# An FFT and two expert layers on one core: half of the first stage's input without halves, its loads joined, the first weight loaded earlier

## The chip, the core and the metric

The kernel runs on one core of a Trainium2 chip. The core has five engines that run beside each other and meet through semaphores: PE (TensorE, the matmuls; PEld are its weight loads), DVE (VectorE), ACT (ScalarE), POOL (GpSimd) and SP (SyncE, which here only issues DMAs). The metric is device time in microseconds; lower is better.

## What is computed

An FFT over tokens and features of x, of which the real part is kept, goes through two expert layers one behind the other, all in float32:

```python
X = np.fft.fft(np.fft.fft(x, axis=1), axis=2).real      # x: 2 x 3008 x 256
h = X.reshape(6016, 256) @ w_in                         # w_in: 256 x 2048
g = np.maximum(h, 0.0) + alpha * np.minimum(h, 0.0)
Y = g @ w_out                                           # w_out: 2048 x 256
h = Y @ w_in2
out = (h / (1.0 + np.exp(-h))) @ w_out2
```

## The kernel before, in words

The FFT over 3008 = 47 x 64 tokens is done in two stages. Stage A is a product with the table `cat` over 47 points. Its result goes through DRAM (`tmid`), which turns it, and stage B is a product with `cbt` over 64 points. The FFT over features is folded into the first weight: `mix_w` multiplies `w_in` with the table `cwt` and gives `wa`. The tokens that come out are cut in six groups c = 0 to 5. The body then runs 16 steps for each group (`step1`: product with `wa`, activation, product with `wo1`) and then the second layer in the same manner. A plan written out by hand (lists of step numbers such as STAGE_A, STAGE_B, WOUT) says at which step what side work is issued; the instructions of each engine run in the order in which the program issues them.

Products use a fast float32 format (float32r) of lower precision. To keep float32, an operand is split: `hi` is a rounded copy (ACT), `lo` is the rest (DVE or POOL), and three matmuls give hi x hi, lo x hi and hi x lo. An operand that stays plain float32 needs no halves and one matmul; psB, psW and psP are made so.

The change lies in the prologue for group 0, ahead of step 1. It goes thus:

- PE runs ten idle matmuls on zeros (`spin(SPIN[0])`). SP issues the loads of x in eight parts `xr[i]` of 96 x 1024 and of the table `ca`.
- For each part i: `split` makes xh (ACT) and xl (DVE) one part ahead, `stage_a` does two halves of three matmuls each (L304 to L306), ACT copies the first half out of PSUM to `evs[i]`, DVE the second (L893, L895). Then the entry `QUEUE[i]` says which DMAs follow: "s" saves rows of tmid for the first third (L313), "l" loads rows back into `ur` (L846; the name pq in the trace, since ur lies in pq of the last group), "w" and "b" load the tables cwt and cbt from ACT's queue, "p" begins the conversion of a first-layer weight: it issues its load (L165), and the next `next(first[0])` its ACT steps (L193, L194) and DVE steps (L199, L201, L203), which turn a pair of 32-bit words into a float32. "o" loads a raw w_out.
- `ur` holds 128 partitions; the even rows (e = 0) and the odd rows (e = 1) of a part are loaded by DMAs of their own, the odd ones in two large DMAs at the end.
- Behind the stage: 14 idle matmuls, the mixing of weight 0 (psW, L452, and psS, L458), 8 idle matmuls, stage B for group 0 (psB, L917: eight products for the even rows, then eight for the odd ones), the row product of POOL (L912) and its sum on PE (psP, L928), the conversion of weight 1, and step 1 (psh, L495).

SP issues in order: while a DMA waits for a semaphore, all that stand behind it wait too. A load waits until the saves that it reads have landed.

Of the kernel before, what the change touches and what calls it, by code (L numbers as in the profile page):

```python
# [9 lines left out]
F32 = mybir.dt.float32  # L10
# [4 lines left out]
ALU = mybir.AluOpType  # L15
# [7 lines left out]
NP1 = 48  # L23
# [4 lines left out]
CK = 8  # L28
# [49 lines left out]
def kernel(  # L78
# [13 lines left out]
    nc = tc.nc  # L92
    V, A, G, T = nc.vector, nc.scalar, nc.gpsimd, nc.tensor
# [206 lines left out]
    def stage_a(hi, lo, tag="x"):  # L300

        t = ptile([P, 4, P], "psA", tag)
        ps = t[:2 * NP1]
        T.matmul(ps, cat[:, 0, :], hi, start=True, stop=False)  # L304
        T.matmul(ps, cat[:, 1, :], hi, start=False, stop=False)
        T.matmul(ps, cat[:, 0, :], lo, start=False, stop=True)  # L306
        return ps
# [455 lines left out]
    def start_win2():  # L763
# [15 lines left out]
    T2 = 14, 16, 19, 22, 50, 51, 52, 53, 54, 56, 58  # L779
    SUB = G  # L780
    STEP2 = [0] + [NC * NF + 56 * c for c in range(NC - 1)]
    SPIN = 10, 14, 8

    QUEUE = ((("s", 0, 8),), (("s", 8, 16),), (("s", 16, 24), ("w",), ("b",)), (("s", 24, 32), ("p", 0)),
             (("l", 0, 16, 0), ("s", 32, 40)), (("l", 16, 32, 0), ("s", 40, 48)), (("s", 48, 56), ("l", 32, 48, 0)),
             (("s", 56, 60), ("s", 60, 64), ("l", 48, 56, 0), ("l", 56, 64, 0), ("l", 0, 32, 1), ("l", 32, 64, 1),
              ("a",), ("p", 1), ("o",)))
    FIRST = 6
    WARM = {}

    RAWS = {"o0": (0, "wA2"), "o1": (1, "wA2"), "i2": (0, "px1"), "i3": (1, "px1"), "i4": (0, "wA3"), "i5": (1, "wA3"),
# [9 lines left out]
    with tc.manual_schedule():  # L801
# [39 lines left out]

        first = [narrow_win(p) for p in range(2)]

        def load_ur(a, b, e):
            dst = ur[2 * a:2 * b, e * CK:(e + 1) * CK]
            nc.sync.dma_start(dst, tmid[0][a:b].rearrange("n (c e m) j -> (n c) e m j", c=2, e=2)[:, e])  # L846

        def save(a, b):
            i = a // NX
# [3 lines left out]
        def move(what):  # L853
            kind, *at = what
            if kind == "s":
                save(*at)
            elif kind == "l":
                load_ur(*at)
            elif kind == "w":
                A.dma_start(cwt.rearrange("p k e j -> p (k e j)"), cw)  # L860
            elif kind == "b":
                A.dma_start(cbt.rearrange("p e k -> p (e k)"), cb)
            elif kind == "a":
                nc.sync.dma_start(al, alpha)
            elif kind == "p":
                next(first[at[0]])
            elif kind == "o":
                load_raw("o", 0)

        sp = {}  # L870

        def split(i):
            hi = wtile([2 * NP1, NX, P], F32R, "xh0", "gh")
            lo = wtile([2 * NP1, NX, P], F32R, "xl0", "gl")
            A.activation(hi, xr[i], AF.Copy)
            V.tensor_tensor(lo, xr[i], f32(hi), op=ALU.subtract)
            sp[i] = hi, lo

        V.tensor_copy(*con)
        split(0)  # L880
        evs = []
        for i in range(nx):
            if i + 1 < nx:
                split(i + 1)
            if i % 2 == 0:
                t = keep.tile([2 * NP1, 2, NX, P], F32, name="ev0", tag=("px2", "px3", "px4", "px6")[i // 2])
            evs.append(t[:, i % 2])
            hi, lo = sp.pop(i)
            for h in range(2):
                sl = slice(h * 4, h * 4 + 4)  # L890
                ps = stage_a(hi[:, sl], lo[:, sl], "x" if (2 * i + h) % 4 == 3 else "h")
                if h == 0:
                    A.activation(evs[i][:, sl], ps, AF.Copy)  # L893
                else:
                    V.tensor_copy(evs[i][:, sl], ps)  # L895
            for what in QUEUE[i]:
                move(what)
            if i == FIRST:
                next(first[0])
# [166 lines left out]
```

## Time and profile before

| | us |
|---|---|
| median of 3 runs | 994.22 |
| lowest, highest | 994.04, 995.43 |
| the profiled execution | 997.01 |
| its span, first to last instruction | 995.2 |

The profile is of one execution of its own, a little longer than the median. The page gives the busy time of each engine; the timeline gives each instruction's start (us from the span's start), its duration, and in brackets how long its engine stood idle before it and what released it. A matmul's end is modelled, so the distance between two starts tells more than a duration. DMAs show when they were issued, and in the view of DMA issues how long until they landed.

### The profile page before, as it was taken

Reading aid. Unit: us, or ns where it says so; the run is one execution under the profiler, and the core shown is the slowest. Engines: PE = TensorE matmul, PEld = TensorE weight load, DVE = VectorE, ACT = ScalarE, POOL = GpSimd, SP = SyncE. Lnnn points to the kernel's source line nnn. Section 1 sums busy time; section 2 is a strip of 40 time slices with the busy share of each in tenths; the row PEclk is TensorE's granted clock in tenths of the full one; section 3 lists DMA queues with packets and bytes.
Section 4 is the critical chain, followed back from the end, with each engine's and each line's share of the span. In section 5 each row is a group of like instructions: output and inputs, shape, how many; then the busy total and the mean of one; then the engine's idle time right before and its main releaser. Section 6 shows DMA issues by size and latency. Waiting matters only on the chain. (4 is left out here: it accounts for less than half of the span.)

```text
span 995.2 us, 12396 instructions
## 1 busy us (share of the span) xinstructions
PE 963.0 (97%) x4316; PEld 792.8 (80%) x4316; DVE 733.0 (74%) x1103; ACT 597.1 (60%) x1002; POOL 519.3 (52%) x328
## 2 busy tenths in 40 slices
PE   8799999999999999999999999999999999999998
PEld 5677778878888878777787788888888888888886
DVE  6698877678777789988999875576566566657654
ACT  6566566665555556666787666565565566566554
POOL 0155657765545556887987654254253354335222
PEclk9899999999999999999999999999999999999999
DMA  8921123221011010110122020000001001001001
GB/s 224 318 83 38 41 75 90 76 63 51 1 53 54 1 53 22 42 64 26 39 68 81 1 82 1 1 22 22 1 1 43 1 1 40 1 0 43 1 1 43
DMA packets 35950, 46.43 MB, mean 47 GB/s; under 512 B 3408, under 2 KB 22192, under 8 KB 35632
## 3 DMA queue, kind: packets, MB, share of 16 engines
q1 hardware_dynamic: 35600, 45.32, 14.6%
q8 instruction: 34, 0.56, 0.2%
q10 hardware_dynamic: 288, 0.33, 0.1%
q14 instruction: 28, 0.23, 0.1%
HBM read 32.11 MB, written 13.52 MB: 46 GB/s over the span
## 5 line engine op out<-in xcount | busy, mean ns | idle before, releaser
L679 DVE TENSOR_TENSOR ring<-ring,psh 128x512 f32<-128x512 f32 (+1 forms) x336 | 221.7, 674 | 154.2 <-PE psh L658 141.2
L726 PE MATMUL pso<-ghl,wAo 128*128 128x512 f32 (+1 forms) x1152 | 312.3, 387 | 1.7 <-POOL ghl L670 1.7
L525 POOL TENSOR_TENSOR gl<-r,gh 128x1024 fp32r<-128x1024 f32 (+1 forms) x96 | 231.5, 2412 | 150.2 <-ACT gh L524 107.0
L658 PE MATMUL psh<-ts,wi 128*128 128x512 f32 (+1 forms) x1008 | 281.4, 387 | 2.5 <-DVE ring L679 1.5
L670 POOL TENSOR_TENSOR ghl<-ring,ghl 128x512 fp32r<-128x512 f32 (+1 forms) x96 | 139.3, 1451 | 249.6 <-ACT ghl L665 169.9
L726 PEld LDWEIGHTS pso<-ghl,wAo 128*128 128x128 f32 x1152 | 216.7, 188 | 44.9 <-POOL ghl L670 2.5
L682 ACT ACTIVATE ring<-ring 128x512 f32<-128x512 f32 (+1 forms) x192 | 119.5, 623 | 173.6 <-DVE ring L679 171.6
L658 PEld LDWEIGHTS psh<-ts,wi 128*128 128x128 f32 x1008 | 189.3, 188 | 40.4 <-DVE ring L679 2.2
L540 PE MATMUL pso<-gh,wo_o 128*128 128x512 f32 (+1 forms) x768 | 189.8, 388 | 2.4 <-POOL wo_o L221 2.3
L495 PE MATMUL psh<-pq,wa 128*128 128x512 f32 (+1 forms) x576 | 168.1, 400 | 5.6 <-DVE r L509 5.5
L540 PEld LDWEIGHTS pso<-gh,wo_o 128*128 128x128 f32 x768 | 144.2, 188 | 32.2 <-POOL wo_o L221 4.0
L509 DVE SCALAR_TENSOR_TENSOR r<-r,al,psh 128x512 f32<-128x512 f32 (+1 forms) x192 | 132.9, 734 | 15.7 <-ACT r L505 4.6
L524 ACT ACTIVATE gh<-r 128x1024 fp32r<-128x1024 f32 (+1 forms) x96 | 100.3, 1045 | 65.0 <-DVE r L509 64.6
L495 PEld LDWEIGHTS psh<-pq,wa 128*128 128x128 f32 x576 | 105.2, 189 | 30.9 <-DVE r L509 11.9
L665 ACT ACTIVATE ghl<-ring 128x512 fp32r<-128x512 f32 (+1 forms) x192 | 119.1, 620 | 6.3 <-PE psh L658 0.4
L505 ACT ACTIVATE r<-psh 128x512 f32<-128x512 f32 (+1 forms) x96 | 56.5, 589 | 94.9 <-DVE psh L504 94.9
L504 DVE TENSOR_TENSOR psh<-h,psh 128x512 f32<-128x512 f32 (+1 forms) x96 | 65.9, 686 | 55.5 <-PE psh L495 51.5
L540 PE MATMUL pso<-gl,wo_o 128*128 128x512 f32 (+1 forms) x384 | 104.0, 392 | 2.4 <-POOL gl L525 2.4
L540 PEld LDWEIGHTS pso<-gl,wo_o 128*128 128x128 f32 x384 | 72.5, 190 | 18.5 <-POOL gl L525 4.1
L670 DVE TENSOR_TENSOR ghl<-ring,ghl 128x512 fp32r<-128x512 f32 (+1 forms) x96 | 76.8, 800 | 2.7 <-ACT ghl L665 2.7
L503 DVE SCALAR_TENSOR_TENSOR h<-pb,wst,psh 128x512 f32<-128x512 f32 (+1 forms) x96 | 69.9, 729 | 2.7 <-PE psh L495 2.7
L506 DVE TENSOR_TENSOR psh<-h,psh 128x512 f32<-128x512 f32 (+1 forms) x96 | 65.2, 679 | 0.0
(90 smaller groups left out, 699.4 us busy)
## 6 DMA issues: line engine op xcount, KB each, us to landing
raw<-in_w_in SPq DMA_DIRECT2D x16, 512.0 KB, 5.3
raw<-in_w_out SPq DMA_DIRECT2D x16, 512.0 KB, 4.0
ur<-tmid SPq DMA_DIRECT2D x20, 256.0 KB, 3.8
out_dram<-ob SPq DMA_DIRECT2D x16, 256.0 KB, 2.1
tmid<-ev SPq DMA_DIRECT2D x50, 64.0 KB, 1.8
x<-in_x SPq DMA_DIRECT2D x8, 384.0 KB, 8.6
xr<-in_x SPq DMA_DIRECT2D x16, 192.0 KB, 2.4
tmid<-ev SPq DMA_DIRECT2D x23, 128.0 KB, 4.6
```

Source lines behind the costliest of these rows:

```text
L495: T.matmul(t[:, :w], wa[q][:, mm, eo, a, :], pq[c][:, 2 * eo + bb, :w], start=n == 0, stop=n == 2)
L503: V.scalar_tensor_tensor(t[:, :w], pb[c][:, :w], wst[:, m, 0:1], ps[0][:, :w], op0=ALU.mult, op1=ALU.add)
L509: V.scalar_tensor_tensor(r[:, s, :w], r[:, s, :w], al[:, m:m + 1], ps[s][:, :w], op0=ALU.mult, op1=ALU.add)
L524: A.activation(hi[:, :, :w], r[:, :, :w], AF.Copy)
L525: G.tensor_tensor(lo[:, :, :w], r[:, :, :w], f32(hi[:, :, :w]), op=ALU.subtract)
L540: T.matmul(po[c][s][k][:, :w], wo1[q][:, mm, a, k * P:(k + 1) * P], g[:, s, :w], start=m == 0 and a == 0 and g is hi, stop=m == NF - 1 and ...
L658: T.matmul(bank[j][:, :w], wi2[p][:, FORMS[j], a], t[:, :w], start=a == 0 and t is hi, stop=t is lo)
L665: A.activation(outs[p, i][:, 0, :w], g[:, :w], AF.Copy)
L670: eng.tensor_tensor(hl[:, 1, :w], g[:, :w], f32(hl[:, 0, :w]), op=ALU.subtract)
L679: V.tensor_tensor(dst[:, :w], a[:, :w], bank[j][:, :w], op=ALU.add)
L682: A.activation(a[:, :w], a[:, :w], AF.Silu)
L726: T.matmul(po[c, 2][s][k][:, :w], wo2[q][:, mm + m, a, k * P:(k + 1) * P], outs[p, i][:, g, :w], start=p == 0 and i < 2 and a == 0 and g == 0,
```

## The change

Five things in the prologue, and nothing behind it:

- The even parts of x (0, 2, 4, 6) are no longer split. `stage_a` gets `lo = None` and does one float32 matmul with the table `full`, the sum of both halves of the table, which DVE adds up once. The odd parts are split as before, while the part ahead of them is on.
- The load of the first weight is issued directly behind x, ahead of all saves (`move(("p", 0))`). Its conversion follows part 7 and not part 6 (`FIRST`).
- A load of `ur` brings even and odd rows by one transfer, so rows of 8 KB; there are five loads and not seven.
- The loads stand elsewhere in `QUEUE`.
- The idle matmuls behind the stage are 11 and 2 instead of 14 and 8.

```diff
         t = ptile([P, 4, P], "psA", tag)
         ps = t[:2 * NP1]
+        if lo is None:
+            T.matmul(ps, full, hi, start=True, stop=True)
+            return ps
         T.matmul(ps, cat[:, 0, :], hi, start=True, stop=False)
...
-    SPIN = 10, 14, 8
-
-    QUEUE = ((("s", 0, 8),), (("s", 8, 16),), (("s", 16, 24), ("w",), ("b",)), (("s", 24, 32), ("p", 0)),
-             (("l", 0, 16, 0), ("s", 32, 40)), (("l", 16, 32, 0), ("s", 40, 48)), (("s", 48, 56), ("l", 32, 48, 0)),
-             (("s", 56, 60), ("s", 60, 64), ("l", 48, 56, 0), ("l", 56, 64, 0), ("l", 0, 32, 1), ("l", 32, 64, 1),
+    SPIN = 10, 11, 2
+
+    QUEUE = ((("s", 0, 8),), (("s", 8, 16),), (("s", 16, 24), ("w",), ("b",)), (("s", 24, 32),),
+             (("l", 0, 16), ("s", 32, 40)), (("s", 40, 48), ("l", 16, 32)), (("s", 48, 56),),
+             (("s", 56, 60), ("s", 60, 64), ("l", 32, 48), ("l", 48, 56), ("l", 56, 64),
               ("a",), ("p", 1), ("o",)))
-    FIRST = 6
+    FIRST = 7
...
-        def load_ur(a, b, e):
-            dst = ur[2 * a:2 * b, e * CK:(e + 1) * CK]
-            nc.sync.dma_start(dst, tmid[0][a:b].rearrange("n (c e m) j -> (n c) e m j", c=2, e=2)[:, e])
+        def load_ur(a, b, e=None):
+            src = tmid[0][a:b].rearrange("n (c m) j -> (n c) m j", c=2)
+            sl = slice(0, 2 * CK) if e is None else slice(e * CK, (e + 1) * CK)
+            nc.sync.dma_start(ur[2 * a:2 * b, sl], src[:, sl])
...
+        move(("p", 0))
         sp = {}
...
+        full = pf.tile([2 * NP1, 96], F32, name="full")
+        V.tensor_tensor(full, con[1][:, :96], con[1][:, 96:], op=ALU.add)
         V.tensor_copy(*con)
-        split(0)
         evs = []
         for i in range(nx):
-            if i + 1 < nx:
+            if i % 2 == 0:
                 split(i + 1)
...
-            hi, lo = sp.pop(i)
+
+            hi, lo = sp.pop(i, (xr[i], None))
             for h in range(2):
                 sl = slice(h * 4, h * 4 + 4)
-                ps = stage_a(hi[:, sl], lo[:, sl], "x" if (2 * i + h) % 4 == 3 else "h")
+                ps = stage_a(hi[:, sl], lo if lo is None else lo[:, sl], "x" if (2 * i + h) % 4 == 3 else "h")
```

On PE, from the first idle matmuls into stage A (psA the result, x a part of x, xh and xl its halves, cat and full the tables), before:

```order
L812 MATMUL idle<-zero 128x512 x10
L304 MATMUL psA<-xh_127,cat 96x512
L305 MATMUL psA<-xh_127,cat 96x512
L306 MATMUL psA<-xl_128,cat 96x512
L304 MATMUL psA<-xh_127,cat 96x512
L305 MATMUL psA<-xh_127,cat 96x512
L306 MATMUL psA<-xl_128,cat 96x512
```

and now:

```order
L815 MATMUL idle<-zero 128x512 x10
L305 MATMUL psA<-x_112,full 96x512 x2
L307 MATMUL psA<-xh_131,cat 96x512
L308 MATMUL psA<-xh_131,cat 96x512
L309 MATMUL psA<-xl_132,cat 96x512
L307 MATMUL psA<-xh_131,cat 96x512
L308 MATMUL psA<-xh_131,cat 96x512
L309 MATMUL psA<-xl_132,cat 96x512
```

The six matmuls of part 0 became two, which read x itself; those of part 1 stay.

On SP, from the end of the loads of x to the last load of ur (tmid<-ev are saves, pq<-tmid the loads of ur, raw the first weight), before:

```order
L313 DMA tmid_69<-ev_135 32x8x128 x2
L313 DMA tmid_69<-ev_166 32x8x128 x2
L165 DMA raw_195<-in_w_in 128x2x512
L846 DMA pq_111<-tmid_69 32x1024
L313 DMA tmid_69<-ev_201 32x8x128
L846 DMA pq_111<-tmid_69 32x1024
L313 DMA tmid_69<-ev_201 32x8x128
L313 DMA tmid_69<-ev_234 32x8x128
L846 DMA pq_111<-tmid_69 32x1024
L313 DMA tmid_69<-ev_234 32x4x128 x2
L846 DMA pq_111<-tmid_69 16x1024 x2
L846 DMA pq_111<-tmid_69 64x1024 x2
```

and now:

```order
L165 DMA raw_126<-in_w_in 128x2x512
L316 DMA tmid_69<-ev_135 32x8x128 x2
L316 DMA tmid_69<-ev_158 32x8x128 x2
L850 DMA pq_111<-tmid_69 32x2048
L316 DMA tmid_69<-ev_183 32x8x128 x2
L850 DMA pq_111<-tmid_69 32x2048
L316 DMA tmid_69<-ev_208 32x8x128
L316 DMA tmid_69<-ev_208 32x4x128 x2
L850 DMA pq_111<-tmid_69 32x2048
L850 DMA pq_111<-tmid_69 16x2048 x2
```

The weight moved ahead of four saves, and the two loads of odd rows at the end are gone, in exchange for rows of twice the length.

On ACT, the end of stage A (xh the high half of the last part, ev the copies out of PSUM, wq and raw the first weight), before:

```order
L875 ACTIVATE xh_230<-x_123 96x1024
L893 ACTIVATE ev_234<-psA 96x512
L193 ACTIVATE wq<-raw_195 128x512
L194 ACTIVATE raw_195<-raw_195 128x512
L893 ACTIVATE ev_234<-psA 96x512
```

and now:

```order
L880 ACTIVATE xh_204<-x_123 96x1024
L900 ACTIVATE ev_208<-psA 96x512 x2
L193 ACTIVATE wq<-raw_126 128x512
L194 ACTIVATE raw_126<-raw_126 128x512
L457 ACTIVATE wa_274<-psW 128x2x2x128
```

The two conversion steps moved behind the last copy out of PSUM.

## Rows read from the trace of the kernel before

**Rows 1.** The page: busy time of each engine, with its share of the span.
```profile
PE 963.0 (97%) x4316; PEld 792.8 (80%) x4316; DVE 733.0 (74%) x1103; ACT 597.1 (60%) x1002; POOL 519.3 (52%) x328
```

**Rows 2.** Timeline of stage A (start, duration, engine, line, operation), one part's pace.
```profile
14.89 1.21 DVE L876 TENSOR_TENSOR xl<-x,xh 96x1024 fp32r<-96x1024 f32 x1
...
16.03 0.68 DVE L895 COPY ev<-psA 96x512 f32<-96x512 f32 x1
...
16.47 0.39 PE L304 MATMUL psA<-xh,cat 96*96 96x512 f32 x1
...
16.63 1.21 DVE L876 TENSOR_TENSOR xl<-x,xh 96x1024 fp32r<-96x1024 f32 x1
16.70 0.39 PE L305 MATMUL psA<-xh,cat 96*96 96x512 f32 x1
```

**Rows 3.** Timeline of the head; and a window of stage A (last column GB/s).
```profile
6.40 1.06 ACT L875 ACTIVATE xh<-x 96x1024 fp32r<-96x1024 f32 x1 [1.02 <-DMA x<-in_x]
...
7.49 1.22 DVE L876 TENSOR_TENSOR xl<-x,xh 96x1024 fp32r<-96x1024 f32 x1 [0.86 <-ACT xh L875]
...
8.00:10.00 2.00, 1.55 (x8) 0.89 (x6) 2.00 (x3) 1.77 (x3) 0.00 (x0) 1.00 1.04 250
```

**Rows 4.** Timeline from the end of stage A to psB.
```profile
20.40 0.40 PE L306 MATMUL psA<-xl,cat 96*96 96x512 f32 x1
...
22.72 0.69 DVE L203 SCALAR_TENSOR_TENSOR wq<-raw,wq 128x512 int32<-128x512 int32 x1
...
23.85 1.89 PE L452 MATMUL psW<-wq,cwt 128*128 128x256 f32 x8
...
25.93 2.11 PE L812 MATMUL idle<-zero 128*128 128x512 f32 x8
...
27.88 3.68 PE L917 MATMUL psB<-cbt,pq 128*128 128x64 f32 x32
```

**Rows 5.** SP's issues in the timeline; then single issues, with us to landing last.
```profile
22.50 3.02 SPq L846 DMA_DIRECT2D pq<-tmid  x4
...
raw<-in_w_in SPq DMA_DIRECT2D x1, 512.0 KB, 4.3
...
pq<-tmid SPq DMA_DIRECT2D x1, 128.0 KB, 2.3
...
tmid<-ev SPq DMA_DIRECT2D x1, 64.0 KB, 2.1
```

**Rows 6.** Timeline of POOL: what the row product waited for.
```profile
29.37 1.06 POOL L912 TENSOR_TENSOR row<-pq,cbt 128x512 f32<-128x512 f32 x1 [28.92 <-DMA pq<-tmid]
```

**Rows 7.** Timeline of PE behind psB.
```profile
31.40 1.08 PE L928 MATMUL psP<-row,ones 128*128 128x512 f32 x2
31.91 1.88 PE L495 MATMUL psh<-pq,wa 128*128 128x482 f32 x6
```

**Rows 8.** Timeline of ACT and DVE in step 1.
```profile
35.37 0.67 ACT L193 ACTIVATE wq<-raw 128x512 f32<-128x512 f32 x1 [1.12 <-DMA raw<-in_w_in]
...
38.22 1.35 DVE L509 SCALAR_TENSOR_TENSOR r<-r,al,psh 128x482 f32<-128x482 f32 x2 [0.48 <-ACT r L505]
```

**Rows 9.** Windows: length, busy PE, PEld, DVE, ACT, POOL; granted clock, DMA share, GB/s.
```profile
17.80:20.40 2.60, 2.39 (x9) 1.46 (x10) 2.37 (x4) 1.66 (x4) 0.00 (x0) 1.00 0.93 319
20.40:22.50 2.10, 2.10 (x11) 1.70 (x10) 1.53 (x3) 1.05 (x3) 0.00 (x0) 1.00 0.47 117
...
26.20:29.30 3.10, 3.10 (x22) 2.74 (x21) 0.69 (x1) 0.23 (x2) 0.00 (x0) 1.00 0.94 244
39.90:42.10 2.20, 0.02 (x1) 0.00 (x0) 2.20 (x4) 0.71 (x1) 1.41 (x1) 1.00 0.98 361
44.10:49.40 5.30, 5.28 (x14) 4.30 (x15) 5.09 (x9) 4.21 (x7) 1.29 (x1) 0.54 1.05 382
```

**Rows 10.** A longer window (columns as above), and a wait of PE at its end.
```profile
39.50:67.20 27.70, 22.40 (x95) 18.22 (x94) 26.53 (x42) 16.63 (x28) 13.53 (x7) 0.88 0.59 211
...
67.71 0.61 PE L458 MATMUL psS<-ones,wq 128*128 128x2 f32 x4 [1.36 <-DVE pq L365]
```

## The prediction

> **What bounds the kernel now.** I read the page first, then the timeline of the first 70 us, then waits and windows in it. The page says that TensorE (PE) is busy for 97% of the span [rows 1]: the body is a chain of matmuls in a fixed order, and the change touches none of it. What it can move is the time at which that chain begins. So the question is one of the prologue: when does step 1 start (before: 31.9 us, [rows 7]), and does a shift there reach the end.
>
> The timeline of the first stage shows its pace. Two DVE subtractions of two successive parts of x start 1.74 us apart (14.89 and 16.63), and DVE has no gap between them: 1.21 for the low half, 0.68 for the copy out of PSUM. ACT has 1.06 for the high half [rows 3] and a shorter copy. PE issues a matmul of 512 columns every 0.23 us, so six of a part are 1.39 [rows 2]. So the stage is bound by DVE, and PE has some 0.35 us of slack in each part. x itself is on time: a part of 384 KB takes 1.6 us at 250 GB/s, part 1 is there at 6.4, so the last one comes near 6.4 + 6 x 1.57 = 15.8 [rows 3].
>
> Behind the stage three things run side by side. (a) DVE converts the first weight to float32, ends at 22.72 + 0.69 = 23.41, PE mixes it from 23.85, and then eight idle matmuls fill PE until psB begins at 27.88 [rows 4]. (b) The rows of tmid are saved, and loaded again turned: the last four loads are issued from 22.50 to 25.52 [rows 5], and the last one lands at about 29.2, where POOL is released [rows 6]. The second half of psB (the odd rows) begins about 16 x 0.112 = 1.8 us after the first, at 29.6, so (b) just fits behind (a). (c) The other raw weights come behind the loads; ACT waits 1.12 us for one of them at 35.37 [rows 8].
>
> **The change, part by part.**
>
> *Float32 parts.* Four of eight parts lose their ACT half (1.06) and their DVE subtraction (1.21). A pair of parts then asks of DVE 1.21 + 2 x 0.68 = 2.57, of ACT 1.06 and two copies of less than 0.68, both below PE. For PE the three fast matmuls of each half become one float32 matmul, which stands in the trace as two records. Its price is not in the stage before. Nearest rows: psW has eight records of 256 columns in 1.89 us including the tail, 0.215 apart, so 0.43 for 512 columns and 0.86 for a matmul; psP, the only one of 512 columns, shows 31.40 to its second record and step 1 behind it, 1.08 with the tail, at most 0.97 without it [rows 4, 7]. I take 0.86 (many records back to back) and keep 0.97 as the upper end. Below nothing is excluded: three fast ones take 0.69. So a pair is 2 x 0.86 + 1.39 = 3.11 us on PE, against 3.47 now on DVE. PE becomes the bound of this stage.
>
> The Trainium skill, page "FP8 and Floating Point Precision", section "TensorE Precision Notes", says that true FP32 takes four passes through the array, which speaks against this edit: four passes in place of three. By it a matmul is about 4 x 0.23 = 0.92 us, an estimate, between my two ends, and the sum below would lose 0.3 us. The records at 0.215 for 256 columns agree with it.
>
> The end of the stage: part 1 is still split, and its low half ends at 7.49 + 1.22 = 8.71 as now, because x sets that [rows 3]. Four matmuls of that part remain (to 9.67), then three pairs of 3.11 = 9.33, and some 0.6 where the odd parts' low halves come late (ACT does xh behind a copy, DVE xl behind that; stepping through all three engines I get 0.3, 0.1 and 0.25 for parts 3, 5 and 7). The stage ends at 19.6 and its last matmul starts at 19.4 instead of 20.40. From there copy and conversion go on as now (20.40 to 23.41 is 3.0): 22.4. **Gain 1.0 us.** The added DVE sum for the float32 table (96 columns) is less than a copy of 512 (0.68) and lies ahead of part 1's wait for x: nothing, while x1 lands at 6.4 [rows 3].
>
> *First weight behind x.* It is issued at about 8 us (behind x it first waits for the third part's semaphore) and lands 1.3 to 2 us behind the last x, near 17.3, instead of 19.7 [rows 5]. ACT then converts after the last copy and not ahead of it: now its two steps stand between the last two copies. No gain of its own: DVE's copy sets the end of conversion either way. The cost lies on the DMA queue: 512 KB now stand in front of every save. The saves of parts 0 to 3, issued from 9.4 on and held behind x anyway, come 1.3 to 2 us later; SP stands at the first load until about 18.4, and the saves of parts 4 and 5, ready by then, queue behind SP.
>
> *Idle matmuls.* 14 to 11: hidden, since they end at 19.6 + 2.4 = 22.0, ahead of the weight at 22.4. 8 to 2: six of 0.215 go from PE's path, **gain 1.3 us.** PE is ready for psB at 27.88 - 1.0 - 1.3 = 25.6.
>
> *Merged loads.* Now the last loads are four, the even rows of parts 6 and 7 and then two of 256 KB with all odd rows, whose data run until 29. After, each load brings both rows, and at the end stand 256 KB and two of 128 KB. The last save is issued when the last copy ends (about 20.7). A small save lands 2.1 us after its issue, a load of 128 KB 2.3 us [rows 5]: 20.7 + 2.1 + 2.3 = 25.1 if the queue is clear. It is not quite: from 19.4 on about 1 MB passes (saves 4 to 7, two loads); at the 319 GB/s of the stretch from 17.8 to 20.4 [rows 9] that is 3.2 us, so the last save lands nearer 23.5 and the last load at 25.8. Best case 25.1; worst, at the 244 GB/s of the stretch 26.2 to 29.3 [rows 9], about 1 us more, 26.8. I take 25.7, next to the 25.6 of PE.
>
> All of psB now waits for all loads. 25.7 against 27.88: **psB starts 2.2 us earlier**, and psP, POOL's row product (1.06 us beside 3.6 us of psB, hidden) and step 1 with it.
>
> *Raw weights.* They follow the loads, which end 3.5 us earlier, so ACT's wait of 1.12 goes. Its value: the DVE operation behind it waited 0.48 for ACT's Relu [rows 8]. **Gain 0.45.**
>
> Sum: 2.2 (of the 2.3 that PE gains, 1.0 + 1.3, the loads leave so much) + 0.45 = 2.65; I take 2.6. Does it reach the end? From 39.5 to 67.2 us DVE is busy for 26.53 of 27.70, and at 67.71 PE waits 1.36 for it; DMA is busy for 0.59 of that stretch, so the transfers have room [rows 10]. Nothing there hangs on the absolute time, so the whole order moves. The profiled execution took 997.01 with a span of 995.2; it would be 994.4. It lies 2.8 above the median of 994.22, which becomes **991.6**.
>
> **The rivals.**
>
> *Late loads (no measurable change).* The two round trips, save then load, set psB, and PE's idle matmuls were the only thing cut. For it: 512 KB more in front of the saves, and the load's path has at best 0.6 us of room. Against: DMA moves only 117 GB/s from 20.4 to 22.5 [rows 9], so there is room to catch up. At 27 to 28 us the gain is 0.35 to 1.35: 992.9 to 993.9.
>
> *Float32 is dear (on the edge of no change).* The edit then doesn't do what it says. At 0.97 a matmul a pair is 3.33, the six on the path cost 0.66 more, the stage gains 0.35 and not 1.0, psB starts at 26.25: 994.22 - 1.6 - 0.45 = 992.2, on the edge.
>
> *The clock falls (slower).* Only two idle matmuls stand between the mix and psB, where eight bridge it now, so PE stands still from 25.7 until the loads are there. The windows show what an idle stretch can cost: PE stands still from 39.9, the granted clock is full up to 42.1, and from 44.1, where work begins again, to 49.4 it is 0.54, its lower level of 1.2 GHz but for the end [rows 9]. I put the point from which this rival decides at an idle stretch as long as the one ahead of that fall, 2.2 us: loads that land after 27.9 or so. Price: psB 3.6, psP 0.9 and six matmuls of step 1 (1.3) at half speed, up to 5.8 more, of which I take 3.5: 994.22 - 0.4 + 3.5 = 997.3. The Trainium skill, page "TensorE: Matmul & The Clock Gate", section "Why this matters for your kernels", warns of idle gaps between bursts for this reason; the trace agrees, with the 0.54 behind the stretch without work.
>
> **How the numbers follow.** A measurement of this kernel tells about 0.2%, 2 us, from no change; so faster means under 992.2, slower over 996.2. Forecast 991.6 and what lies near or under it: 57%. Late loads 25%, dear float32 10% (half of it on either side of the bound), the clock 8%. Faster 0.62, same 0.30, slower 0.08. Low end: loads at 25.1, a smaller loss between parts (0.5 less) and the full 1.1 of ACT's wait, 994.22 - 4.0 = 990.2. High end: late loads to the last, 994.2; beyond it only the clock.
>
> **What would show it.** Records of the float32 matmul 0.43 apart; the last matmul of the stage near 19.4; the end of the first conversion at 22.4; psB at 25.7, waiting for a load or for nothing; the first PE matmul of step 1 at 29.7 instead of 31.9; no DMA wait on ACT near 32; the PE idle row of 67.71 near 65. Wrong it would be if psB waits on a load beyond 27, if the clock shows half before 35 us, or if the start moves by 2.6 and the PE row at 67 doesn't.

## The result: slower by 0.6%

| | before | after |
|---|---|---|
| median, us | 994.83 (4 runs) | 1000.73 (4 runs) |
| lowest to highest | 994.04 to 995.87 | 1000.15 to 1004.05 |
| the profiled execution, its span | 997.01, 995.2 | 1000.58, 998.1 |

The ratio of after to before is 1.0062, with a 95% interval of 1.0045 to 1.0079. The forecast was 991.6; the time lies outside its range and beyond even the rival that was to be slower (997.3).

The work is the same. The page of after, busy times with their shares of the span, stands beside [rows 1]:

```profile
PE 963.3 (97%) x4299; PEld 791.4 (79%) x4299; DVE 729.1 (73%) x1100; ACT 593.1 (59%) x998; POOL 519.8 (52%) x328
```

PE is busy for 0.3 us more than in [rows 1], in fewer instructions. So the place to look at is the prologue. Timeline of after, the first part that is split and the end of stage A (start, duration, engine, line, operation; in brackets idle time and what ended it):

```profile
6.88 1.06 ACT L880 ACTIVATE xh<-x 96x1024 fp32r<-96x1024 f32 x1 [4.87 <-DMA x<-in_x]
...
14.07 0.16 PEld L305 LDWEIGHTS psA<-x,full 96*96 96x96 f32 x1 [0.27 <-issue]
14.50 0.16 PEld L305 LDWEIGHTS psA<-x,full 96*96 96x96 f32 x1 [0.27 <-issue]
...
17.23 1.06 ACT L880 ACTIVATE xh<-x 96x1024 fp32r<-96x1024 f32 x1
...
18.32 1.22 DVE L881 TENSOR_TENSOR xl<-x,xh 96x1024 fp32r<-96x1024 f32 x1 [0.44 <-ACT xh L880]
...
19.60 0.47 PE L309 MATMUL psA<-xl,cat 96*96 96x512 f32 x1 [0.26 <-DVE xl L881]
...
20.38 0.40 PE L309 MATMUL psA<-xl,cat 96*96 96x512 f32 x1
...
20.81 0.69 DVE L902 COPY ev<-psA 96x512 f32<-96x512 f32 x1 [0.66 <-PE psA L309]
```

A float32 record is 0.43 us from the next (14.07 and 14.50, the weight loads of two records), the price that the prediction took. Yet the last matmul starts at 20.38 as in [rows 4] (20.40). The last part of x landed at 17.1 in this execution, and from there one chain runs to the end: high half, low half, matmul. The stage was late before that: part 1 was there at 6.88 and not at 6.40 as in [rows 3], when the weight had not even been issued (8.62).

SP's issues in after (the x at the end is a count), and single DMAs with their size and the us from issue to landing:

```profile
19.81 0.31 SPq L850 DMA_DIRECT2D pq<-tmid  x1
...
21.70 1.67 SPq L316 DMA_DIRECT2D tmid<-ev  x3
23.72 2.65 SPq L850 DMA_DIRECT2D pq<-tmid  x3
```

```profile
raw<-in_w_in SPq DMA_DIRECT2D x1, 512.0 KB, 10.4
...
tmid<-ev SPq DMA_DIRECT2D x1, 128.0 KB, 9.1
...
tmid<-ev SPq DMA_DIRECT2D x2, 64.0 KB, 3.4
```

The weight was issued at 8.62 and the first save at 10.35. They landed at 19.1 and 19.4, some 2 us behind x. SP stood at the first load of ur until 19.81; the last save was issued at 22.79, and the last load landed at 29.34 and not at 25.7.

PE behind the stage in after, against [rows 4, 7]:

```profile
25.63 0.71 PE L815 MATMUL idle<-zero 128*128 128x512 f32 x2
...
29.53 5.62 PE L924 MATMUL psB<-cbt,pq 128*128 128x64 f32 x32 [3.19 <-issue]
...
34.94 2.02 PE L935 MATMUL psP<-row,ones 128*128 128x512 f32 x2
...
35.97 2.82 PE L498 MATMUL psh<-pq,wa 128*128 128x482 f32 x6
```

The view names no releaser for psB; the last load landed at 29.34, just ahead of it. psB is 5.62 us long where it was 3.68, and step 1 starts 6.44 us behind the start of psB where that distance was 4.03. The windows of after tell why (length, busy PE, PEld, DVE, ACT, POOL, granted clock, DMA share, GB/s):

```profile
26.00:28.00 2.00, 0.34 (x2) 0.00 (x0) 0.69 (x1) 0.13 (x2) 0.00 (x0) 1.00 0.78 144
28.00:30.00 2.00, 0.47 (x5) 0.50 (x5) 0.00 (x0) 0.00 (x0) 0.54 (x1) 1.00 0.95 247
30.00:32.00 2.00, 2.00 (x17) 2.00 (x16) 0.00 (x0) 0.23 (x2) 0.52 (x1) 0.78 1.05 398
32.00:34.00 2.00, 2.00 (x11) 2.00 (x11) 0.79 (x3) 0.47 (x2) 0.00 (x0) 0.50 1.03 316
34.00:36.00 2.00, 2.00 (x9) 1.48 (x8) 0.08 (x1) 0.70 (x3) 0.00 (x0) 0.50 1.09 340
36.00:38.00 2.00, 2.00 (x6) 1.27 (x5) 0.71 (x3) 1.00 (x3) 0.00 (x0) 0.51 1.02 270
```

PE does next to nothing from 26.3 to 29.5. When work begins, the granted clock is still full, then it falls to the lower level, 1.2 GHz, in the middle of psB and stays there up to 38. So step 1 starts 4.06 us later than in [rows 7]: 1.65 from the start of psB and 2.41 from the clock.

### The profile page after: what moved, and what is told of

Same layout as the page of the kernel before. It is cut to its first block, busy times and chain, and to the rows that moved or that the text cites. A ratio compares the mean times of both kernels' runs of the same rounds, so it can differ in the third digit from the quotient of the medians.

```text
span 998.1 us, 12349 instructions
## 1 busy us (share of the span) xinstructions
PE 963.3 (97%) x4299; PEld 791.4 (79%) x4299; DVE 729.1 (73%) x1100; ACT 593.1 (59%) x998; POOL 519.8 (52%) x328
## 3 DMA queue, kind: packets, MB, share of 16 engines
q1 hardware_dynamic: 35440, 45.32, 14.9%
## 5 line engine op out<-in xcount | busy, mean ns | idle before, releaser
L498 PEld LDWEIGHTS psh<-pq,wa 128*128 128x128 f32 x576 | 105.5, 190 | 31.2 <-DVE r L512 11.6
L543 PEld LDWEIGHTS pso<-gl,wo_o 128*128 128x128 f32 x384 | 72.5, 190 | 18.4 <-POOL gl L528 4.1
```

Source lines behind the costliest of these rows:

```text
L498: T.matmul(t[:, :w], wa[q][:, mm, eo, a, :], pq[c][:, 2 * eo + bb, :w], start=n == 0, stop=n == 2)
L543: T.matmul(po[c][s][k][:, :w], wo1[q][:, mm, a, k * P:(k + 1) * P], g[:, s, :w], start=m == 0 and a == 0 and g is hi, stop=m == NF - 1 and ...
```

## The experiments

Theory: the weight's load directly behind x pushes the saves and so the loads of ur back, PE stands still ahead of psB, and the granted clock falls there. Rivals: the float32 matmuls; the joined loads; the smaller number of idle matmuls alone. Each ratio is to runs of the kernel before on the same chip; over all of them the kernel before has a median of 995.27 (103 runs, 992.36 to 998.82). The changed kernel itself has only its four runs; a difference to it in us compares medians taken at different times, between which the median of before moved from 994.83 to 995.38.

Landing and issue times in us, from the profile of each kernel; the last two columns are the starts of psB and of step 1:

| kernel | last x lands | first save lands | first load issued | last save issued | last load lands | psB | step 1 |
|---|---|---|---|---|---|---|---|
| before | 15.6 | 15.9 | 17.0 | 22.0 | 29.2 | 27.9 | 31.9 |
| after | 17.1 | 19.4 | 19.8 | 22.8 | 29.3 | 29.5 | 36.0 |
| a_spin18 | 16.1 | 18.5 | 18.8 | 21.9 | 28.2 | 29.8 | 33.9 |
| a_wlate | 16.0 | 16.3 | 17.5 | 21.2 | 27.0 | 27.2 | 31.3 |
| a_wlate_spin8 | 15.3 | 15.6 | 16.5 | 20.7 | 26.4 | 26.7 | 30.8 |
| a_split | 16.2 | 18.6 | 18.9 | 23.5 | 30.3 | 27.7 | 34.9 |
| a_savefirst | 15.8 | 18.1 | 21.2 | 20.8 | 29.0 | 29.2 | 37.0 |
| a_wlater | 16.3 | 16.5 | 16.8 | 21.0 | 29.5 | 31.5 | 35.5 |
| b_w | 16.6 | 19.0 | 19.4 | 24.0 | 30.9 | 28.4 | 34.8 |
| b_merged | 15.9 | 16.3 | 17.5 | 23.4 | 29.1 | 29.3 | 33.5 |
| b_order_joined | 14.2 | 14.5 | 15.7 | 21.7 | 27.5 | 27.7 | 31.8 |
| b_order_split | 16.0 | 16.1 | 17.2 | 22.0 | 28.7 | 28.3 | 32.3 |
| b_f32 | 15.2 | 15.5 | 16.5 | 21.4 | 28.3 | 27.2 | 31.2 |
| b_spin2 | 15.6 | 15.8 | 16.8 | 22.0 | 28.9 | 26.4 | 32.1 |
| f32_spin6 | 15.5 | 15.7 | 16.6 | 21.9 | 28.7 | 26.6 | 31.1 |
| f32_early | 14.9 | 15.2 | 16.1 | 21.0 | 27.2 | 26.1 | 30.1 |

Names that begin with a_ are the changed kernel with one edit (two in a_wlate_spin8 and a_wlater, idle matmuls being the second), those with b_ the kernel before with one edit; f32_spin6 and f32_early are the kernel before with more than one.

### Is it PE's idle stretch? a_spin18

```diff
-    SPIN = 10, 11, 2
+    SPIN = 10, 11, 18
```

> The changed kernel with 18 idle matmuls ahead of psB instead of 2, nothing else. In its profile psB waits for the last load of ur until 29.5 us, PE stands still for 3.2 us ahead of it, and the granted clock is half from about 31 to 38. Theory 'the clock falls': the idle matmuls end at about 29.5, the clock stays full, psB's 32 records stand 0.056 to 0.112 apart instead of twice that, step 1 starts near 33.4 instead of 36.0, and the time falls by 2.5 to 4 us from the changed kernel's 1000.7, to 996.7 to 998.2. Theory 'the loads alone': the clock costs nothing that other work does not hide, step 1 stays near 36 or the body takes the gain back, 1000.7 within 1.

Measured: 996.42, ratio 1.0006 (0.9995 to 1.0016): 4.3 us less than after, by nothing but 16 more idle matmuls. PE in a_spin18, and a window:

```profile
25.63 4.37 PE L815 MATMUL idle<-zero 128*128 128x512 f32 x18
29.84 3.68 PE L924 MATMUL psB<-cbt,pq 128*128 128x64 f32 x32
...
33.87 1.88 PE L498 MATMUL psh<-pq,wa 128*128 128x482 f32 x6
```

```profile
32.00:34.00 2.00, 2.00 (x17) 1.76 (x16) 0.79 (x3) 0.91 (x5) 0.00 (x0) 1.00 1.04 345
```

psB starts later than in after, at the full clock, and step 1 starts 2.1 us earlier. The mean granted clock over the span, averaged over the runs, is 0.9953 against 0.9903 in after (before: 0.9949). So the idle stretch is the larger part of the loss; this is shown, since the two kernels' runs do not overlap (994.42 to 998.19 and 1000.15 to 1004.05).

### The weight's place: b_w, a_wlate, a_wlate_spin8

b_w is the kernel before with the weight's load behind x and nothing else:

```diff
-    QUEUE = ((("s", 0, 8),), (("s", 8, 16),), (("s", 16, 24), ("w",), ("b",)), (("s", 24, 32), ("p", 0)),
+    QUEUE = ((("s", 0, 8),), (("s", 8, 16),), (("s", 16, 24), ("w",), ("b",)), (("s", 24, 32),),
...
+        move(("p", 0))
         sp = {}
```

> The kernel before with the load of the first weight directly behind x and nothing else. Theory 'the weight holds up the saves': the last x lands 1 to 1.5 us later, the last load of ur at about 30.7 instead of 29.2, psB's odd half waits about 1.2 us, time 995.5 to 997. Theory 'the weight only changes places' (the same bytes pass before the last load): loads and time as before, 994.0 to 995.4.

Measured: 997.35, ratio 1.0016 (1.0005 to 1.0027), slower. PE in b_w:

```profile
28.41 1.97 PE L918 MATMUL psB<-cbt,pq 128*128 128x64 f32 x16 [0.21 <-issue]
31.05 2.93 PE L918 MATMUL psB<-cbt,pq 128*128 128x64 f32 x16 [0.67 <-DMA pq<-tmid]
...
34.80 3.40 PE L495 MATMUL psh<-pq,wa 128*128 128x482 f32 x6
```

The last load lands 1.7 us later than before, the second half of psB waits for it, and then runs at the lower clock.

a_wlate is the edit the other way round: the changed kernel with the weight's load at its place of before.

```diff
-    QUEUE = ((("s", 0, 8),), (("s", 8, 16),), (("s", 16, 24), ("w",), ("b",)), (("s", 24, 32),),
+    QUEUE = ((("s", 0, 8),), (("s", 8, 16),), (("s", 16, 24), ("w",), ("b",)), (("s", 24, 32), ("p", 0)),
...
-        move(("p", 0))
```

> The changed kernel with the load of the first weight back in its old place, behind the saves of parts 0 to 3; float32 parts, joined loads and idle matmuls stay. Theory 'the weight holds up the saves': the last part of x lands near 15.7 instead of 17.1, the first load is issued near 17 instead of 19.8, the last one lands at about 27 instead of 29.3, PE stands still for about 1 us only, the clock stays full, and the time is 993 to 995. Theory 'the joined loads are slow': the last load still lands at 28.5 or later, the clock falls, and the time is 999 or more.

Measured: 995.8, ratio 1.0003 (0.9993 to 1.0013): 4.9 us less than after, and a little above the 993 to 995 expected. Five profiles have the weight behind x (after, a_spin18, a_split, a_savefirst, b_w): in them the first save lands 2.3 to 2.4 us behind the last part of x, in all others 0.2 to 0.4 us. The first load of ur is issued 2.35 us earlier in a_wlate than in after, and the last one lands 2.39 us earlier: the chain of loads moves as a whole with its first link. Not all of that is the weight, since x was there at 16.0 in a_wlate and at 17.1 in after. a_spin18 has the weight behind x and its last part at 16.1: against it the first load is issued 1.3 us earlier (17.46 for 18.78) and the last one lands 1.2 earlier (26.95 for 28.16). PE still stood for a moment in a_wlate:

```profile
27.15 3.76 PE L923 MATMUL psB<-cbt,pq 128*128 128x64 f32 x32 [1.17 <-DMA pq<-tmid]
```

a_wlate_spin8 covers that too:

```diff
-    SPIN = 10, 11, 2
+    SPIN = 10, 11, 8
```

> The changed kernel with the weight's load at its place of before (behind the save of part 3) and 8 idle matmuls ahead of psB in place of 2. With 2 of them (a_wlate) psB waited for the last load until 27.15 and PE stood still for some 1.7 us. If that idle stretch costs by the granted clock, the idle matmuls alone bring the time from 995.8 to 994 or 994.5, with psB still at 27.1 to 27.4 and a higher mean granted clock over the runs. If the clock's falls have nothing to do with it, the time stays at 995.8 or rises by the few tenths by which psB is later.

Measured: 994.68, ratio 0.9997 (0.9986 to 1.0009). Against a_wlate that is 1.1 us less, with step 1 no later, as the theory had it; the intervals of the two overlap, so it is not shown.

What the transfers did from 18 to 20 us, one row each of before, after, a_wlate and a_savefirst (which follows):

```profile
18.00:20.00 2.00, 1.89 (x8) 1.09 (x9) 2.00 (x3) 1.06 (x3) 0.00 (x0) 1.00 0.99 344
```

```profile
18.00:20.00 2.00, 1.74 (x7) 0.68 (x6) 1.68 (x2) 0.77 (x2) 0.00 (x0) 1.00 0.49 145
```

```profile
18.00:20.00 2.00, 1.99 (x7) 0.89 (x6) 1.79 (x2) 0.79 (x2) 0.00 (x0) 1.00 0.90 294
```

```profile
18.00:20.00 2.00, 1.99 (x9) 1.01 (x8) 1.45 (x2) 0.78 (x3) 0.00 (x0) 1.00 0.66 158
```

A load has to wait for the saves that it reads. At its old place the weight, which depends on nothing, moves in that time: 344 and 294 GB/s. Behind x it is through by then, and the transfer engines stand half idle (0.49; 0.66 in a_savefirst). The kernel before has such a stretch too, but later, when its first loads are through: 0.47 from 20.4 to 22.5 [rows 9]. The Trainium skill, page "DMA: Bandwidth & Descriptors", section "Queues, rings and completion order", says that each engine takes its descriptors in the order of the ring; the trace agrees, with saves that were issued behind the weight and landed 2.4 us behind x instead of 0.3.

### By which way? a_savefirst

All saves of the first third ahead of all loads, the weight still behind x:

```diff
-             (("l", 0, 16), ("s", 32, 40)), (("s", 40, 48), ("l", 16, 32)), (("s", 48, 56),),
-             (("s", 56, 60), ("s", 60, 64), ("l", 32, 48), ("l", 48, 56), ("l", 56, 64),
+             (("s", 32, 40),), (("s", 40, 48),), (("s", 48, 56),),
+             (("s", 56, 60), ("s", 60, 64), ("l", 0, 16), ("l", 16, 32), ("l", 32, 48), ("l", 48, 56), ("l", 56, 64),
```

> The changed kernel with all saves of the first third ahead of all loads of ur on SP; the weight's load stays directly behind x, 2 idle matmuls. If SP standing at the first load is what delays the last saves, the last one is now issued near 21 to 21.5 and not at 22.8, lands near 23.5, and the last load lands at 26.5 to 27.5: PE stands still for 1 to 2 us and the time is 996 to 997.5. If the 512 KB themselves fill the path to the end, the last load still lands at 28.5 to 29.5 and the time is 999 to 1001.

Measured: 1000.73, ratio 1.0047 (1.0031 to 1.0062). The last save was issued at 20.82 and landed 1.6 us later, so SP no longer held it up. Still the last load landed at 28.96:

```profile
tmid<-ev SPq DMA_DIRECT2D x1, 64.0 KB, 1.6
```

```profile
29.16 7.06 PE L924 MATMUL psB<-cbt,pq 128*128 128x64 f32 x32 [3.52 <-DMA pq<-tmid]
```

So SP's queue alone is not the cause: the loads, 1 MB that now begin at 21.2, take 7.8 us. That they would be done by 27.5 was wrong. It is no proof that the 512 KB fill the path either, since in 20 to 22 us the DMA share is 0.55. The run can't tell the two apart further: it takes SP's wait away and also issues the first load 1.4 us later than after does. What would fit all kernels of this order is that the loads have to begin early, while the last parts of the stage are still on; no run shows that by itself.

### The other parts alone

**b_f32**, float32 matmuls for the even parts in the kernel before:

```diff
+        if lo is None:
+            T.matmul(ps, full, hi, start=True, stop=True)
+            return ps
...
-            if i + 1 < nx:
+            if i % 2 == 0:
                 split(i + 1)
```

> The kernel before with the float32 matmul for parts 0, 2, 4 and 6 alone; queue, loads, weight and idle matmuls as before. If a pair of parts costs 3.11 us on PE and nothing else sets the stage, its last matmul starts at 19.4 and the first conversion ends at 22.4. If the low half of the odd parts, which hangs on x and on ACT, sets it, the last matmul starts at 19.9 to 20.1 and the conversion ends at 22.9 to 23.1. In either case 8 idle matmuls and the loads hold psB near 27.2 to 27.9, and the time is that of before within 1 us: 994 to 995.5. If the float32 matmul itself is what made the changed kernel slower, this one is slower by some 5 us (near 1000).

Measured: 993.82, ratio 0.999 (0.9978 to 1.0003), the lowest median of all. Last matmul at 19.72. In the six profiles with float32 parts and the weight at its old place or later, the last matmul of the stage starts at 19.78 on average (19.56 to 20.01), in the six with neither the float32 parts nor the moved weight at 20.66 (20.08 to 21.05): a gain of 0.9 us.

**b_spin2**, the idle matmuls alone:

```diff
-    SPIN = 10, 14, 8
+    SPIN = 10, 11, 2
```

> The kernel before with 11 and 2 idle matmuls in place of 14 and 8, and nothing else. PE is ready for psB near 26.2 and not 27.9; the even rows are there by then (26.1), the odd ones not before 29.2 to 30, so its second half stands still for 1 to 1.5 us and step 1 begins where it did, near 32. If the loads set the end, the time is that of before: 995 to 995.8. If an idle stretch of 1 to 1.5 us between the halves is enough to bring the clock down, it is 997 to 998. If the prediction's first step were right (six idle matmuls are 1.3 us on the path), it is 994.

Measured: 995.88, ratio 1.0014 (1.0003 to 1.0025). PE in b_spin2, and a window:

```profile
26.44 1.89 PE L917 MATMUL psB<-cbt,pq 128*128 128x64 f32 x16
29.05 2.25 PE L917 MATMUL psB<-cbt,pq 128*128 128x64 f32 x16 [0.72 <-DMA pq<-tmid]
```

```profile
32.00:34.00 2.00, 2.00 (x5) 1.29 (x4) 0.79 (x3) 0.89 (x4) 0.00 (x0) 0.50 1.01 297
```

The first half of psB comes 1.4 us earlier than in [rows 4], the second waits for the last load, the clock is at its lower level soon after, and step 1 starts at 32.1. The 1.3 us of idle matmuls were no gain.

**b_merged**, the joined loads alone, in the order of before:

```diff
-             (("l", 0, 16, 0), ("s", 32, 40)), (("l", 16, 32, 0), ("s", 40, 48)), (("s", 48, 56), ("l", 32, 48, 0)),
+             (("l", 0, 16), ("s", 32, 40)), (("l", 16, 32), ("s", 40, 48)), (("s", 48, 56), ("l", 32, 48)),
...
```

> The kernel before with each load of ur bringing even and odd rows, five loads in place of seven, and nothing else; 14 and 8 idle matmuls. If the joined loads are a gain of their own, the last one lands some 2 us earlier than the 29.2 of before, near 27.3, the raw weights follow earlier and ACT's wait for one near 35 goes; psB stays near 27.9 behind the idle matmuls, so the time falls by 0.4 at the most: 994.4 to 995.3. If rows of 8 KB are what delayed the changed kernel's loads, the last one lands at 29 or later, psB waits for it and the clock may fall: 998 to 1000.

Measured: 999.91, ratio 1.0041 (1.0023 to 1.0059). This was not foreseen as the likelier case. The last load lands at 29.1 as before, but now all of psB waits for it:

```profile
29.34 3.76 PE L918 MATMUL psB<-cbt,pq 128*128 128x64 f32 x32 [0.67 <-issue]
```

In [rows 4] psB began with the even rows at 27.88, while the odd ones came. The start of psB explains 1.5 of the 4.5 us; the mean granted clock of its runs is 0.9919, and the profile of its one execution shows no fall ahead of 43 us, so where the rest went is not shown.

**b_order_joined** and **b_order_split** have the order of the changed kernel (the third load behind the last save), with joined and with separate loads (the diff is that of the separate ones):

```diff
-             (("l", 0, 16, 0), ("s", 32, 40)), (("l", 16, 32, 0), ("s", 40, 48)), (("s", 48, 56), ("l", 32, 48, 0)),
-             (("s", 56, 60), ("s", 60, 64), ("l", 48, 56, 0), ("l", 56, 64, 0), ("l", 0, 32, 1), ("l", 32, 64, 1),
+             (("l", 0, 16, 0), ("s", 32, 40)), (("s", 40, 48), ("l", 16, 32, 0)), (("s", 48, 56),),
+             (("s", 56, 60), ("s", 60, 64), ("l", 32, 48, 0), ("l", 48, 56, 0), ("l", 56, 64, 0), ("l", 0, 32, 1), ("l", 32, 64, 1),
```

> The kernel before with the changed kernel's order on SP (the third load of ur behind the last save) and its joined loads; the weight at its place of before, no float32 matmul, 14 and 8 idle matmuls. If the load ahead of the last saves made b_merged slow, the last load lands at 26.5 to 27.5 here, psB begins near 27.9 behind the idle matmuls and the time is that of before: 994.5 to 995.5. If joined rows are slow in themselves, it lands at 29, psB waits for it and the time is 998 to 1000.

> As b_order_joined, but with even and odd rows loaded apart as before, seven loads. If order is all that counts, the last load lands at 28.3 to 28.8, half a us ahead of before, and the time is that of before: 994.5 to 995.5, equal to b_order_joined. If joining is a gain of its own, the last load here is 1.5 to 2 us later than in b_order_joined, hidden behind the first half of psB.

Measured: 995.64, ratio 0.9999 (0.999 to 1.0009), and 995.26, ratio 1.0006 (0.9995 to 1.0018). So joined loads do no harm where the third load stands behind the last save: that save is issued at 21.7, against 23.4 in b_merged. Nor are they a gain: x was there 1.8 us earlier in the execution of b_order_joined, and its last load lands 1.2 us earlier.

**a_split**, the changed kernel with the separate loads and their order of before:

```diff
-             (("l", 0, 16), ("s", 32, 40)), (("s", 40, 48), ("l", 16, 32)), (("s", 48, 56),),
+             (("l", 0, 16, 0), ("s", 32, 40)), (("l", 16, 32, 0), ("s", 40, 48)), (("s", 48, 56), ("l", 32, 48, 0)),
...
```

> The changed kernel with the loads of ur in their old form and order (even rows, then odd rows in two DMAs at the end); the weight directly behind x, float32 parts and 2 idle matmuls stay. Theory 'the weight holds up the saves': the last load lands at 29 to 30 all the same, psB's odd half waits for it, time 998 to 1000. Theory 'the joined loads are slow': the even rows are there at 26.5, the odd ones at 28, the clock stays full, time 993 to 995.5.

Measured: 999.23, ratio 1.0036 (1.0021 to 1.005). Without the joined loads and their order the changed kernel stays slow; the last load lands at 30.3 and the clock falls at 30.2, so the joined loads are not what made it slow.

**a_wlater**, the weight's load behind the save of part 4, and 4 idle matmuls:

```diff
-             (("l", 0, 16), ("s", 32, 40)), (("s", 40, 48), ("l", 16, 32)), (("s", 48, 56),),
+             (("l", 0, 16), ("s", 32, 40), ("p", 0)), (("s", 40, 48), ("l", 16, 32)), (("s", 48, 56),),
...
-        move(("p", 0))
```

> The changed kernel with the first weight's load issued behind the save of part 4 (two places behind the first load of ur) and four idle matmuls ahead of psB. If 512 KB ahead of the saves is the failed step, the first load of ur is issued near 17, the last one lands at 26 to 27, PE is without work for less than 1 us ahead of psB, step 1 starts at 30.5 to 31.5 and the granted clock stays full up to there: 992.5 to 995. The cost is that the weight lands near 20 to 21, the conversion then ends at 23 to 23.5. If the joined loads or the float32 matmuls are the cause, the loads land at 29 as in the changed kernel, and the time is 999 to 1001.

Measured: 998.39, ratio 1.0026 (1.0002 to 1.005). The expectation was wrong: among the loads the weight took from 17.75 to 23.93 to land, and PE waited for its conversion:

```profile
26.68 2.49 PE L455 MATMUL psW<-wq,cwt 128*128 128x256 f32 x8 [3.92 <-DVE wq L203]
```

The weight has a place that is too early and one that is too late; that of before, behind the save of part 3, lies between.

### The same program twice, and two versions further: b_again, f32_spin6, f32_early

> The kernel before once more, for a second profile of the same program. If the falls of the granted clock behind the prologue (near 42, 70 and 93 us in the first profile) belong to the order of the work, the same stretches are at half here. If they hang on where the clock's own count happens to stand, one or two of them are missing or stand elsewhere, and the span differs by 1 to 3 us from 995.2.

The kernel before once more: span 992.8 where it was 995.2. Three windows of the first profile and then of this one:

```profile
41.00:49.00 8.00, 4.88 (x12) 3.96 (x13) 7.80 (x10) 3.81 (x7) 3.20 (x2) 0.57 1.05 389
68.00:74.00 6.00, 6.00 (x22) 5.02 (x23) 4.57 (x8) 3.36 (x8) 2.67 (x2) 0.72 0.00 0
92.00:98.00 6.00, 5.58 (x20) 4.76 (x21) 4.72 (x10) 2.40 (x5) 3.38 (x2) 0.72 0.04 13
```

```profile
41.00:49.00 8.00, 5.47 (x19) 4.26 (x18) 7.82 (x11) 3.82 (x8) 3.61 (x2) 0.79 1.05 390
68.00:74.00 6.00, 6.00 (x30) 5.27 (x31) 4.78 (x9) 4.81 (x10) 3.32 (x3) 1.00 0.00 1
92.00:98.00 6.00, 6.00 (x29) 5.18 (x29) 5.11 (x9) 4.94 (x9) 3.32 (x3) 1.00 0.00 0
```

Step 1 began 0.6 us later in b_again, yet its span is 2.4 us shorter: two falls of the clock that the first profile has are missing. Behind the prologue the falls differ from execution to execution of one program, and a shift of the start by 1 us is small beside that.

f32_spin6 is b_f32 with `SPIN = 10, 11, 6`; f32_early has `SPIN = 10, 11, 5` and an earlier load of odd rows:

```diff
-             (("l", 0, 16, 0), ("s", 32, 40)), (("l", 16, 32, 0), ("s", 40, 48)), (("s", 48, 56), ("l", 32, 48, 0)),
+             (("l", 0, 16, 0), ("s", 32, 40)), (("l", 16, 32, 0), ("s", 40, 48), ("l", 0, 32, 1)), (("s", 48, 56), ("l", 32, 48, 0)),
-             (("s", 56, 60), ("s", 60, 64), ("l", 48, 56, 0), ("l", 56, 64, 0), ("l", 0, 32, 1), ("l", 32, 64, 1),
+             (("s", 56, 60), ("s", 60, 64), ("l", 48, 56, 0), ("l", 56, 64, 0), ("l", 32, 64, 1),
```

> The kernel before with the float32 matmul for the even parts of x and 11 and 6 idle matmuls in place of 14 and 8; loads and weight as before. Conversion ends near 22.7, psB begins near 26.4, its second half near 28.2 with the last load (28.3 in b_f32), step 1 near 30.5 against 31.2 in b_f32: 0.7 us less than b_f32, 1.7 less than before, so 993.2 to 993.8, with a granted clock as in b_f32. If the loads land at 29 or later, PE stands still between the halves and the gain is lost: 994 to 995.

> As f32_spin6, with 5 idle matmuls ahead of psB and the load of the odd rows of parts 0 to 3 issued behind the save of part 5, not at the end: behind the last save only 256 KB of odd rows and 128 KB of even ones are left. If the transfers behind the last save set the last load, it lands near 27.2 instead of 28.3, psB begins near 26.2, step 1 near 30.2: 992.8 to 993.5. If the early load only pushes the saves back, the last load stays at 28.3, the second half of psB waits for it and the time is 994 to 995.

Measured: 994.39, ratio 1.0 (0.9988 to 1.0011), and 993.95, ratio 0.9988 (0.9974 to 1.0002). Both are some 0.5 us above the ranges expected for a gain (993.2 to 993.8 and 992.8 to 993.5). In f32_early the last load lands at 27.16, as expected, and step 1 starts at 30.13, the earliest of all:

```profile
26.10 3.68 PE L921 MATMUL psB<-cbt,pq 128*128 128x64 f32 x32
...
30.13 1.88 PE L498 MATMUL psh<-pq,wa 128*128 128x482 f32 x6
```

That is 1.8 us ahead of [rows 7]; the median is 1.15 us below that of before in the same runs, and the interval still holds 1. f32_early and b_f32 beat the changed kernel by 6.8 and 6.9 us; that either beats the kernel before is likely and not shown.

## Why the prediction was wrong

**The bound and the place** held: PE is 97% busy, and most of the loss arises up to step 1 and its first product (below).

**Float32.** Right in price (0.43 a record) and, over the twelve profiles compared under b_f32, nearly in worth: 0.9 us against 1.0. The Trainium skill, page "FP8 and Floating Point Precision", section "TensorE Precision Notes", with its four passes led to an estimate of 0.92 a matmul; the trace shows two records, 0.86. In the changed kernel the gain did not appear, since x came late: part 1 at 6.88 for 6.40, the last part at 17.1 for 15.8. Part 1 counts for no less: in a_spin18 the last part is there at 16.1, but part 1 only at 7.16, and the last matmul starts at 20.37 all the same. The weight, issued at 8.62, can't have held up part 1. With the weight behind it the last part of x is there at 15.8 to 17.1 in five profiles, without at 14.2 to 16.8 in twelve. The ranges overlap, so how much of that the weight does is open.

**The failed step** is the term under "Merged loads": the time from SP's first load of ur to the landing of the last one. The sum has 7.3 us for it (18.4 to 25.7); after, a_spin18, a_wlate and a_wlate_spin8, the four with this order and the float32 parts, all show 9.4 to 9.8, with the weight in either place. Two links of it are too short. Under "First weight behind x" the prediction lets SP stand at the first load and the saves of parts 4 and 5 queue behind it, but then it reckons the last save as issued when the last copy ends, as if SP were free: in after the last copy ends at 21.50 and the save is issued at 22.79, 1.3 us behind it (0.5 in before: 21.53 and 22.03). And from the landing of the last save to that of the last load it takes 2.3 us, the time of one load of 128 KB, though three loads, 512 KB, land there: 3.4 us in after (25.93 to 29.34), 3.4 to 3.9 in the four. No run changes the number of these loads alone, so that they are the reason is argued and not shown. This term was 2.2 us short.

The other 1.4 of the 3.6 us (29.34 for 25.7) is the start of that chain, 19.8 for 18.4. The weight's own price was right there: from the last part of x to the first load the prediction has 2.6 us (15.8 to 18.4), and after shows 2.7. It was x that landed 1.3 late.

**Idle matmuls.** PE was ready when predicted: the last two began at 25.63. But the 1.3 us of them were counted as a gain on PE's path, where the loads stood behind. b_spin2 shows what they are worth alone: no gain, 0.14% slower.

**Merged loads.** "All of psB now waits for all loads" stands in the prediction as a step of the sum, not as a price. In [rows 4, 6] half of psB ran ahead of the odd rows; joined, psB can start earlier only if the last load lands ahead of 27.9.

**The raw weights.** ACT's wait of [rows 8] is gone in after, but step 1 came 4 us later, so it says nothing of the 0.45. b_order_joined says more, where ACT waits for no weight either: the DVE operation of [rows 8] starts at 37.69 there, 5.91 us behind the start of step 1 (31.78), and 6.31 in [rows 7, 8]. That is 0.40 us, near the 0.45 predicted. The time of b_order_joined (0.999 to 1.0009) can't show so little.

**The rival that came true** is "The clock falls", with a chance of 0.08. Its condition, loads later than 27.9, was met, and the fall stood where it said. Its chance was too small because it hung on the mis-sized term. Its time, 997.3, was 3.4 short. psB starts 1.65 later, where the rival added nothing for a later start and took 0.4 off. The fall itself cost 2.41 up to step 1 and 0.45 more up to the first DVE operation on its product (40.20 in after, 35.69 before), 2.9 and not 3.5. That is 4.5 of the 5.9 us between the medians. How the other 1.4 arise isn't settled. The profile of after is of the run with the highest mean clock of its four (0.993; the others have 0.987 to 0.991), and the mean over its first 100 us is 0.93, as in the profile of before. What after pays ahead of step 1, this execution of before pays behind it (0.54 from 44.1, [rows 9]), so two single profiles can't price the falls; the runs can. Their mean clocks, 0.990 in after and 0.995 in before, are about 19 and 10 us at the lower level, an estimate (twice the missing share of the span). Where the other three runs of after have theirs no profile shows.

## What to carry to other kernels

A transfer that depends on nothing belongs in the time in which loads wait for the saves that they read, not ahead of both: there it cost the first load 1.3 us here. When a load stands in a queue, write down the issue time of everything behind it before an end is reckoned from the moment the data are ready, and price the last wait with all the transfers that land in it. And idle matmuls that cover a wait on loads may be cut only after the loads have been shown to land earlier.

## What the runs showed of the hardware

- A stand of PE well under that of [rows 9] came ahead of falls too: 0.72 us in b_spin2 and 0.67 in b_w, between the halves of psB, with the lower level within 2 us. Of eight profiles in which PE stood for over 0.6 us ahead of psB or within it (a_wlater: ahead of the mixing), six show a fall that begins between 28.0 and 31.8 us (a_wlate and b_merged, with 1.17 and 0.67, none); the nine others show none before 34.7, where in a_wlate_spin8 PE has waited 1.96 us for DVE. The Trainium skill's page "TensorE: Matmul & The Clock Gate", section "Why this matters for your kernels", warns of idle gaps between bursts, longer ones than these two; the traces agree for the long ones (3.2 us in after) and show falls behind short ones as well.
- The 8 KB rows of the joined loads took 0.52 us each on average in after (128 of them) and 0.62 in a_savefirst, where all loads come in one burst, the quickest about 0.31. The 4 KB rows of before took 0.23, the quickest about 0.16. So in after and a_savefirst joining rows did not make bytes cheaper.
- The last part of x lands between 14.2 and 17.1 us from one execution to the next. A single profile places such times to no better than 1 us.
